# Decode attention with an MLP beside it: all sixteen K loads issued ahead of the V loads

## The chip, the cores and the metric

The kernel runs on one core of a Trainium2 chip. The metric is the device time of one execution in microseconds (us). Three runs of the kernel before took 236.51, 237.08 and 235.47 us; their median is 236.51 us. A further execution was profiled, and all durations below come from its trace.

## What is computed

The reference takes four tokens (a batch of 4, one position each, width 576), normalises them, and adds three things: the tokens themselves, a sliding-window attention against a K and a V cache, and a small mixer with an MLP. Cut to what matters:

```python
xn = layernorm(x)
# A: 32 query heads, 16 K/V heads, head width 128, window of the last 2048 of 8192 positions
q = (xn @ wq) ...                                # 576 x 4096
scores = einsum("bhqd,bhkd->bhqk", q, k) * Dh**-0.5
o = einsum("bhqk,bhkd->bhqd", softmax(scores), v)
A = o @ wo                                       # 4096 x 576
# B: two small products, then a 576 -> 4608 -> 576 MLP
h = gelu(layernorm(xn) @ w1);  x1 = xn + shift(h) @ w2
B = x1 + gelu(layernorm(x1) @ w3) @ w4
return x + A + B
```

Nearly all bytes are the two cache windows: 16 heads of K and 16 of V, 2 MB each for the four batch rows together. They and the weights make 88.90 MB of transfers in the profiled execution.

## The kernel before

**Work units.** One of the sixteen K/V heads is a group g. Its K tile (all four batch rows, 2048 positions, 128 wide) is one DMA of 2048 KB into one of three slots of `kring` (`NKU = 3`); its V tile is one such DMA into one of four slots of `vring` (`NVU = 4`).

**K stage.** For each group TensorE transposes the 64 blocks of 128x128 of the K tile in eight batches (`pe_T`, L324 to L332, signals `T{8g}` to `T{8g+7}`), ScalarE and VectorE copy the transposed batches out of PSUM (`evac`, L334 to L337), and TensorE multiplies them with the queries (`pe_SC`, L339 to L349). The scores of all sixteen groups gather in one PSUM region, each group's queries padded with zeros, so the softmax starts only when the last group's scores are in.

**Softmax.** A maximum over the scores (L365), four exponentials (L370), and a double transposition of the probabilities (L373, L378, L384 and L386) into the tile `PT`, about 15 us in all. Every PV product needs all of `PT`.

**V stage.** For each group, `pe_PV` (L398 to L408) runs 64 small matmuls with blocks of the V tile as the stationary operand. Beside them lie the mixer (L456 to L484) and, in three pieces, the output projection with `wo` (`pe_AO`, L426). At the end come the MLP's two products, with `w3` (`pe_h2`, L487) and `w4` (`acc_mm`, L424, called from L522).

**Order and queues.** Every engine's program is a list of steps with a hand-given key; the list is sorted by the key (L533) and emitted in that order. All big loads are issued by SyncE (SP) on one DMA queue, in the order of their keys. SP carries out its steps strictly one after the other: before a DMA whose slot or partner is not free, it waits on a semaphore, and nothing behind it is issued meanwhile. The waits around the change are:

- K of group g waits for the last transposition batch of group g-3, whose slot it takes (L209). K of groups 0 to 2 wait for nothing.
- V of groups 0 to 3 wait for the query projection only, since the query weights lie in the V slots at the start (L213). V of group g from 4 on waits for the PV product of group g-4.
- `wo` lands in the K slots and waits for `T127`, the last transposition of the K stage (L220 to L222). `w1` and `w2` follow it with no wait of their own (L223, L224), and then V of groups 4 to 15 (L225), `w3` (L228) and `w4` (L242).

The key of K of group g is g (L217). The key of V of group g below 4 is `G - V_EARLY + g - 0.5` (L219) with `G = 16` and `V_EARLY = 4`, which is 11.5, 12.5, 13.5 and 14.5: V0 stands behind K11, V1 behind K12, V2 behind K13 and V3 behind K14.

Of the kernel before, what the change touches and what calls it, by code (L numbers as in the profile page):

```python
# [14 lines left out]
V_EARLY = 4  # L15
# [21 lines left out]
def bass_parallel_sum__sliding_block_cached__mixer_s_mlp__decode_kernel(  # L37
# [8 lines left out]
    G = Hkv  # L46
# [11 lines left out]
    with ExitStack() as ctx:  # L58
# [95 lines left out]
        def add_dma(pairs, skey, waits=(), key=0.0, engine="sp"):  # L154
            if skey not in S:
                S[skey] = sem("s_" + "_".join(str(k) for k in (skey if isinstance(skey, tuple) else (skey,))))
            dma_count[skey] = dma_count.get(skey, 0) + 16 * len(pairs)

            def emit(e):
                for o_, i_ in pairs:  # L160
                    e.dma_start(o_, i_).then_inc(S[skey], 16)  # L161
            add(engine, emit, waits, None, key)
            return ("dma", skey, dma_count[skey])
# [41 lines left out]
        def kv_src(cache, g):  # L205
            return cache[:, g, Sk - W:Sk, :].rearrange("b (i t) d -> i b (t d)", t=NT)
# [5 lines left out]
        def issue_v(g, key):  # L212
            w = [f"PV{g - NVU}"] if g >= NVU else (["q"] if g < WQ_SLOTS else [])  # L213
            ev_v.append(add_dma([(vring_t[:, g % NVU * UE:(g % NVU + 1) * UE], kv_src(A_v_cache, g))], ("v", g % NVU), w, key))
# [1 line left out]
        for g in range(G):  # L216
            issue_k(g, g)  # L217
        for g in range(V_EARLY):
            issue_v(g, G - V_EARLY + g - 0.5)  # L219
        wo_wait = f"T{8 * (G - 1) + 7}"  # L220
        ev_wo = add_dma([(wo_sb.rearrange("p h r n -> p h (r n)"), A_wo.rearrange("(h p r) n -> p h (r n)", h=8, r=4))],
                        "wo", [wo_wait], KS)  # L222
# [15 lines left out]
        for c in range(8):  # L238
            g = G - NVU + c // 3
# [371 lines left out]
```

## Time and profile before

| what | number |
|---|---|
| median of three runs | 236.51 us |
| the profiled execution, its own time | 236.61 us |
| its span from the first to the last instruction | 234.9 us |
| moved by DMA | 88.90 MB, mean 378 GB/s over the span |
| TensorE busy | 169.7 us (72%) |
| VectorE busy | 74.3 us (32%) |
| ScalarE busy | 61.4 us (26%) |
| mean granted TensorE clock | 0.789 |

The profile gives all instants in us from the start of the span. The profiled execution's own time is 1.71 us longer than its span. Views used below are: the page's 40 equal slices of the span (a digit is a busy share in tenths; the GB/s row is what the DMA engines moved); the timeline of one engine's instructions; the chain of work that ended last, which names at each moment what the end of the program was waiting for; the table of waits; and a table of stretches between given instants, with busy time and count of each engine, the granted TensorE clock, the DMA engines' busy share and GB/s.

### The profile page before, as it was taken

Reading aid. Unit: us, or ns where it says so; the run is one execution under the profiler, and the core shown is the slowest. Engines: PE = TensorE matmul, PEld = TensorE weight load, DVE = VectorE, ACT = ScalarE, POOL = GpSimd, SP = SyncE. Lnnn points to the kernel's source line nnn. Section 1 sums busy time; section 2 is a strip of 40 time slices with the busy share of each in tenths; the row PEclk is TensorE's granted clock in tenths of the full one; section 3 lists DMA queues with packets and bytes.
Section 4 is the critical chain, followed back from the end, with each engine's and each line's share of the span. In section 5 each row is a group of like instructions: output and inputs, shape, how many; then the busy total and the mean of one; then the engine's idle time right before and its main releaser. Section 6 shows DMA issues by size and latency. Waiting matters only on the chain.

```text
span 234.9 us, 6181 instructions
## 1 busy us (share of the span) xinstructions
PE 169.7 (72%) x2917; PEld 126.3 (54%) x2918; DVE 74.3 (32%) x134; ACT 61.4 (26%) x74; POOL 6.1 (3%) x20
## 2 busy tenths in 40 slices
PE   0367999999999958396293479477498334994996
PEld 0355777777777646375161039444466334664753
DVE  4301566666565545143235850041000000000000
ACT  2001555555555534034234570002000000000000
POOL 8100000000000000000000000000000000000000
PEclk9999999999999999769978555555559555575569
DMA  7999999999999999999606997999999999999970
GB/s 258 421 433 435 413 399 385 419 373 407 410 393 399 419 430 424 427 435 426 276 0 224 418 390 307 416 427 438 413 430 438 413 433 424 428 433 393 410 314 10
DMA packets 8577, 88.90 MB, mean 378 GB/s; under 512 B 860, under 2 KB 1256, under 8 KB 3944
## 3 DMA queue, kind: packets, MB, share of 16 engines
q1 hardware_dynamic: 8536, 88.50, 90.9%
q8 instruction: 23, 0.38, 0.6%
q14 instruction: 2, 0.02, 0.0%
q10 hardware_dynamic: 16, 0.01, 0.0%
HBM read 88.49 MB, written 0.00 MB: 377 GB/s over the span
## 4 chain that ended last, share of the span: by engine, by line
DMA 51%; PE 37%; ACT 6%; DVE 3%; SPq 1%; issue 1%
DMA kring<-in_A_k_cache_dram 24%; PE ps L330 19%; DMA vring<-in_A_v_cache_dram 15%; DMA regB<-in_B_w_dram 12%; PE ps L346 6%; PE ps L424 5%; PE ps L403 5%; ACT regB L336 4%; ACT PT L384 1%; DVE PT L386 1%; PE ps L499 1%; SPq L161 1%; DVE rmax L365 1%; DVE regB L373 1%; PE ps L378 1%
## 5 line engine op out<-in xcount | busy, mean ns | idle before, releaser
L330 PE MATMUL ps<-perm_bf,kring 128*128 128x128 bf16 x1024 | 71.5, 229 | 14.9 <-DMA kring<-in_A_k_cache_dram 14.6
L330 PEld LDWEIGHTS ps<-perm_bf,kring 128*128 128x128 bf16 x1024 | 62.1, 103 | 29.4 <-DMA kring<-in_A_k_cache_dram 16.2
L337 DVE COPY regB<-ps 128x1024 bf16<-128x1024 bf16 x80 | 52.5, 687 | 54.9 <-PE ps L330 53.3
L336 ACT ACTIVATE regB<-ps 128x1024 bf16<-128x1024 bf16 x48 | 48.0, 1023 | 70.0 <-PE ps L330 70.0
L403 PE MATMUL ps<-PT,vring 128*128 128x8 bf16 x1024 | 29.2, 168 | 21.5 <-DMA vring<-in_A_v_cache_dram 20.3
L403 PEld LDWEIGHTS ps<-PT,vring 128*128 128x128 bf16 x1024 | 28.2, 103 | 24.8 <-DMA vring<-in_A_v_cache_dram 22.0
L346 PE MATMUL ps<-regB,Qpad 128*32 128x512 bf16 x256 | 18.4, 412 | 3.6 <-ACT regB L336 3.6
L514 ACT ACTIVATE h2T_sb<-ps 128x144 bf16<-128x144 f32 x1 | 0.3, 291 | 56.7 <-PE ps L508 56.7
L438 DVE TENSOR_TENSOR OTn<-ps,rinvB 128x64 bf16<-128x64 f32 (+2 forms) x3 | 0.6, 203 | 44.4 <-PE ps L403 44.4
L424 PE MATMUL ps<-kring,ORT 128*4 128x288 bf16 x64 | 13.4, 393 | 0.3 <-DVE ORT L442 0.3
L424 PE MATMUL ps<-vring,h2T_sb 128*4 128x288 bf16 x72 | 11.8, 339 | 0.5 <-ACT h2T_sb L514 0.5
L346 PEld LDWEIGHTS ps<-regB,Qpad 128*32 128x32 bf16 x256 | 5.6, 100 | 10.3 <-ACT regB L336 4.3
L378 PE MATMUL ps<-regB,permT 32*128 32x512 bf16 x16 | 5.9, 600 | 5.7 <-DVE regB L373 4.1
L424 PEld LDWEIGHTS ps<-kring,ORT 128*4 128x4 bf16 x64 | 7.0, 112 | 5.6 <-DVE ORT L442 0.4
L424 PEld LDWEIGHTS ps<-vring,h2T_sb 128*4 128x4 bf16 x72 | 7.1, 99 | 5.0 <-issue 0.5
L303 PE MATMUL ps<-xnT,vring 128*128 128x4 bf16 x160 | 4.6, 166 | 5.4 <-DMA vring<-in_A_wq_dram 5.4
L529 DVE CAST out_sb<-ps 4x288 bf16<-4x288 f32 x1 | 0.4, 446 | 23.6 <-PE ps L424 23.6
L499 PE MATMUL ps<-x1nT,regB 128*128 128x4 bf16 x144 | 5.0, 172 | 3.3 <-DMA regB<-in_B_w_dram 3.3
L303 PEld LDWEIGHTS ps<-xnT,vring 128*128 128x128 bf16 x160 | 4.4, 104 | 5.5 <-DMA vring<-in_A_wq_dram 5.5
L499 PEld LDWEIGHTS ps<-x1nT,regB 128*128 128x128 bf16 x144 | 4.9, 117 | 3.9 <-DMA regB<-in_B_w_dram 3.4
L378 PEld LDWEIGHTS ps<-regB,permT 32*128 32x128 bf16 x16 | 1.1, 99 | 10.5 <-DVE PT L386 5.3
L268 ACT ACTIVATE sd<-mv 4x1 f32<-4x1 f32 x3 | 0.6, 202 | 21.3 <-DVE mv L266 21.3
(82 smaller groups left out, 63.3 us busy)
## 6 DMA issues: line engine op xcount, KB each, us to landing
kring<-in_A_k_cache_dram SPq DMA_DIRECT2D x16, 2048.0 KB, 8.6
vring<-in_A_v_cache_dram SPq DMA_DIRECT2D x16, 2048.0 KB, 17.6
kring<-in_A_wo_dram SPq DMA_DIRECT2D x1, 4608.0 KB, 13.9
regB<-in_B_w_dram SPq DMA_DIRECT2D x2, 2304.0 KB, 25.8
vring<-in_B_w_dram SPq DMA_DIRECT2D x8, 576.0 KB, 28.4
vring<-in_A_wq_dram SPq DMA_DIRECT2D x2, 2048.0 KB, 9.6
kring<-in_B_w_dram SPq DMA_DIRECT2D x2, 576.0 KB, 15.1
regB<-in_B_w_dram SPq DMA_DIRECT2D x1, 576.0 KB, 29.9
```

The costliest lines, as they stand in the source:

```text
L161: e.dma_start(o_, i_).then_inc(S[skey], 16)
L303: ins = e.matmul(QTps[:, B * h:B * (h + 1)], lhsT=w, rhs=x_, start=(r == 0 and h == 0), stop=(r == 4), skip_group_check=True)
L330: ins = e.transpose(tb[n % NTB][:, t, :], kring[:, g % NKU, 8 * k + t, :], perm_bf[:])
L336: return "act", lambda e: e.activation(out=ktbuf[:, n % NKT], in_=tb[n % NTB], func=ACTF.Copy)
L337: return "dve", lambda e: e.tensor_copy(out=ktbuf[:, n % NKT], in_=tb[n % NTB])
L346: ins = e.matmul(Sps[32 * b:32 * b + 32, c4, :].rearrange("p (t i) -> p t i", t=16), lhsT=Qpad[:, g, b, :], rhs=kt[:, :, b, :], start=(g = ...
L365: add("dve", lambda e: e.tensor_reduce(out=rmax[:], in_=Sps, axis=AX.XY, op=ALU.max), waits=[f"SC{G - 1}"], sig="rmax", key=KS)
L373: add("dve", lambda e, cs=cs: e.transpose(PTc[:, cs], P_sb[:, cs]), waits=[f"exp{q}"], sig=f"PTc{q}", key=KS + 0.2 + 0.01 * q)
L378: add("pe", lambda e, m=m, q=q, b=b: e.matmul(PTps[m % 4], lhsT=permT[32 * b:32 * b + 32, :], rhs=PTc[32 * b:32 * b + 32, 512 * q:512 * q ...
L403: ins = e.matmul(OTps(g)[:, 8 * g:8 * g + 8].rearrange("p (b e) -> p b e", e=2), lhsT=vring[:, g % NVU, t, :], rhs=r_, start=(t == 0), sto ...
L424: return e.matmul(ACC[h], lhsT=lhsT, rhs=rhs, start=start, stop=stop)
L499: ins = e.matmul(H2Tps[:, n, :], lhsT=w3main[:, r, lo:hi:st], rhs=x1nT[:, r, :], start=(r == 0 and n == 0), stop=False, skip_group_check=True)
```

## The change

One line changes. The first four V loads get the keys 16, 17, 18 and 19 in place of 11.5 to 14.5, so that they stand behind K15 (key 15) and ahead of `wo` (key 132). No instruction is added or taken away, no wait, slot or semaphore differs, and the programs of TensorE, VectorE, ScalarE and GpSimd are the same.

```diff
         for g in range(G):
             issue_k(g, g)
         for g in range(V_EARLY):
-            issue_v(g, G - V_EARLY + g - 0.5)
+            issue_v(g, G + g)
         wo_wait = f"T{8 * (G - 1) + 7}"
```

SP's program before, from the query weights to `wo`. The x12 are K0 to K11; `waits prog_pe` is a wait for TensorE's progress.

```order
L161 DMA vring<-in_A_wq_dram 128x8192 x2
L161 DMA vring<-in_A_wq_dram 128x2048
L161 DMA kring<-in_A_k_cache_dram 128x1x8192 x3
L161 DMA kring<-in_A_k_cache_dram 128x1x8192 [waits prog_pe] x9
L161 DMA vring<-in_A_v_cache_dram 128x1x8192
L161 DMA kring<-in_A_k_cache_dram 128x1x8192 [waits prog_pe]
L161 DMA vring<-in_A_v_cache_dram 128x1x8192
L161 DMA kring<-in_A_k_cache_dram 128x1x8192 [waits prog_pe]
L161 DMA vring<-in_A_v_cache_dram 128x1x8192
L161 DMA kring<-in_A_k_cache_dram 128x1x8192 [waits prog_pe]
L161 DMA vring<-in_A_v_cache_dram 128x1x8192
L161 DMA kring<-in_A_k_cache_dram 128x1x8192 [waits prog_pe]
```

The four V loads alternate with K12 to K15. The same place in the changed program, up to the V loads behind `w2`:

```order
L161 DMA kring<-in_A_k_cache_dram 128x1x8192 x3
L161 DMA kring<-in_A_k_cache_dram 128x1x8192 [waits prog_pe] x13
L161 DMA vring<-in_A_v_cache_dram 128x1x8192 x4
L161 DMA kring<-in_A_wo_dram 128x8x2304 [waits prog_pe]
L161 DMA kring<-in_B_w_dram 128x2304
L161 DMA kring<-in_B_w_dram 128x288
L161 DMA kring<-in_B_w_dram 128x2304
L161 DMA kring<-in_B_w_dram 128x288
L161 DMA vring<-in_A_v_cache_dram 128x1x8192 [waits prog_pe] x12
```

K0 to K15 now stand together, and V0 to V3 lie between K15 and `wo`; they still wait for nothing of TensorE's.

## The prediction on record

> **What bounds the kernel now.** I read the page's slices first. One slice is 5.87 us long, and three rows of it, those of the TensorE clock, the DMA share and the GB/s, already tell most of the story.
>
> ```profile
> PEclk9999999999999999769978555555559555575569
> DMA  7999999999999999999606997999999999999970
> GB/s 258 421 433 435 413 399 385 419 373 407 410 393 399 419 430 424 427 435 426 276 0 224 418 390 307 416 427 438 413 430 438 413 433 424 428 433 393 410 314 10
> ```
>
> The DMA engines are busy in nearly every slice, so bytes bound the kernel, but there is a hole around slice 20 (near 120 us) in which nothing moves, and a dent at slice 24. There is also a long stretch, slices 5 to 12, where the engines count as busy and yet move about 400 GB/s and not 425 to 430. The table of stretches puts edges on these.
>
> ```profile
> 20.50:74.81 54.31, 52.33 (x788) 41.31 (x789) 32.71 (x50) 28.75 (x29) 0.00 (x0) 1.00 0.98 400
> 74.81:115.46 40.65, 28.43 (x400) 21.34 (x397) 16.51 (x26) 16.16 (x16) 0.00 (x0) 0.92 1.00 424
> 115.46:125.20 9.74, 6.81 (x80) 4.69 (x80) 3.27 (x5) 3.03 (x3) 0.00 (x0) 0.82 0.02 10
> 125.20:140.74 15.54, 8.47 (x89) 3.04 (x90) 11.10 (x18) 9.40 (x18) 0.00 (x0) 0.58 1.01 390
> 140.74:142.40 1.66, 1.66 (x68) 1.66 (x66) 0.00 (x0) 0.00 (x0) 0.00 (x0) 0.50 0.02 5
> 142.40:216.40 74.00, 48.68 (x1148) 37.70 (x1145) 5.09 (x18) 1.72 (x4) 0.00 (x0) 0.57 1.01 423
> ```
>
> The columns are the stretch and its length, busy us and count of PE, weight loads, DVE, ACT and POOL, then the granted clock, the DMA share and the GB/s. Two stops stand out: 9.74 us at a DMA share of 0.02, and 1.66 us at 0.02. What SP does then tells why.
>
> ```profile
> 74.81 0.53 SPq L161 DMA_DIRECT2D kring<-in_A_k_cache_dram  x1
> 75.39 0.60 SPq L161 DMA_DIRECT2D vring<-in_A_v_cache_dram  x1
> 80.15 0.54 SPq L161 DMA_DIRECT2D kring<-in_A_k_cache_dram  x1
> 85.50 0.54 SPq L161 DMA_DIRECT2D kring<-in_A_k_cache_dram  x1
> 93.14 0.53 SPq L161 DMA_DIRECT2D kring<-in_A_k_cache_dram  x1
> 124.21 0.40 SPq L161 DMA_DIRECT2D kring<-in_A_wo_dram  x1
> 141.11 45.58 SPq L161 DMA_DIRECT2D vring<-in_A_v_cache_dram  x12
> ```
>
> K12 to K15 are issued at 74.81, 80.15, 85.50 and 93.14. Then SP has nothing it may issue until 124.21, when the last transposition is done and `wo` may overwrite the K slots; all four V slots are full by then. And V4 goes out only at 141.11, when the first PV product has freed a slot, a little after the weights have run out at 140.74. The first stop is the costly one, and the chain of work that ended last says what holds `T127` back.
>
> ```profile
> 93.14 24.17 DMA kring<-in_A_k_cache_dram
> 117.36 1.81 PE ps L330 x16
> 123.56 0.63 PE ps L330 x8
> 139.23 3.55 PE ps L403 x128
> 146.84 17.79 DMA vring<-in_A_v_cache_dram
> 187.36 28.98 DMA regB<-in_B_w_dram
> 220.84 11.85 PE ps L424 x72
> ```
>
> K15 takes 24.17 us to arrive, because V1, V2, V3 and two K tiles lie ahead of it in one queue. Only at 117.36, after the queue has run dry, does TensorE get the last K tile; the softmax then runs to 139.23. From there V and w3 loads lead the chain, and the end is 11.85 us of matmuls with `w4`. TensorE's waits for K say the same.
>
> ```profile
> PE ps L330 <- DMA kring<-in_A_k_cache_dram: 1.2, 1, 1.2
> PE ps L330 <- DMA kring<-in_A_k_cache_dram: 13.4, 4, 4.7
> ```
>
> The first row is the window from 20 to 75 us, the second 75 to 125. Up to 75 us TensorE never waits for K but at the start: there it sets the pace, one group per 5.34 us (80.15 less 74.81), and SP issues K as slots come free. From the first early V on, each K tile is late.
>
> **The change, part by part.** No operation is added, so all is a matter of when bytes flow.
>
> *K12 to K15 come early.* K12 still goes out at 74.81, which is the end of group 9. With no V load ahead of it, it should land as those before did:
>
> ```profile
> kring<-in_A_k_cache_dram SPq DMA_DIRECT2D x16, 2048.0 KB, 8.6
> ```
>
> 8.6 us is the median from issue to landing, and a tile is needed two groups after its issue, 10.7 us, so about 2 us are spare. TensorE then keeps its 5.34 us for groups 10 to 15: K13 goes out at 80.15, K14 at 85.50, K15 near 90.84, and `T127` ends at 74.81 + 6 x 5.34 = 106.9 where it now ends at 124.2. TensorE's own 17.3 us are not the gain, since nothing waits for it but `wo` and the softmax.
>
> *V0 to V3 fill the hole.* SP issues them right behind K15, from 91.4 to 93.8 at 0.60 us each; the query projection they wait for is long done. How long do they keep the DMA engines busy? Between 74.81 and 115.46 these moved 40.65 x 0.424 = 17.24 MB, and the same bytes have to flow in the new order. Until K15 starts, TensorE paces them at the 400 GB/s of the first row of stretches. I put that start 1 us behind its issue, 91.84, as `wo` is issued at 124.21 and moves from 125.20. So 17.03 us carry 6.81 MB; the other 10.43 MB run freely.
>
> ```profile
> 80.00:115.00 35.00, 23.47 (x323) 17.58 (x320) 13.40 (x21) 13.20 (x13) 0.00 (x0) 0.90 1.01 427
> ```
>
> At 427 GB/s, the rate of the saturated part, 10.43 MB take 24.4 us, and V3's last bytes flow near 116.3 us. Against 115.46 the pacing **costs 0.85 to 0.96 us** (the second with 424 GB/s: 17.03 x 24 / 424). I take 0.96. The unknown is whether the 400 GB/s is pacing or the price of transposing beside the loads. The 427 row, with TensorE still busy 23.47 of 35 us, is nearer to pacing. If it is contention, V loads up to 106.9 run at 400 too and cost another 15.1 x 27 / 427 = 0.95 us; below nothing this term cannot go, for at best the rate is the free one.
>
> *The first stop goes.* `wo` may be issued from 106.9 on, some 9 us ahead of the end of V3. It queues behind V3 and starts without a pause: **9.74 us gained**. The cover is 9 us thick: if K15 or the last group is later than that, the stop comes back microsecond for microsecond.
>
> *The second stop goes.* PV of group 0 ends, and V4 is issued, 141.11 - 124.21 = 16.9 us after `T127`, so near 123.8 us. The weights `wo`, `w1` and `w2` flow from 116.4 to about 131 (15.54 us or a little less), so V4 is in the queue 7 us before it is needed, V5 to V7 soon after, each a PV product later: **1.66 us gained**. V0 to V3 must have landed for those PV products; the last does near 118.2, as K15's did 1.9 us (117.36 - 115.46) after the stream stopped, and PV0 starts at 106.9 + 139.23 - 124.21 = 121.9. Nothing is late next.
>
> *The starts after the stops go.* A stream that begins in an idle queue is slow at first:
>
> ```profile
> 125.20:126.00 0.80, 0.61 (x12) 0.39 (x16) 0.00 (x0) 0.78 (x2) 0.00 (x0) 1.00 0.99 115
> 126.00:140.00 14.00, 7.11 (x54) 1.91 (x46) 11.10 (x18) 8.23 (x17) 0.00 (x0) 0.56 1.02 408
> 142.40:144.00 1.60, 1.60 (x45) 1.54 (x43) 0.29 (x1) 0.00 (x0) 0.00 (x0) 0.50 1.01 348
> 144.00:216.40 72.40, 47.08 (x1109) 36.17 (x1106) 4.80 (x17) 1.72 (x4) 0.00 (x0) 0.57 1.01 425
> ```
>
> The weights' 15.54 x 0.390 = 6.06 MB at 408 GB/s take 14.9 us, 0.6 less; V4's first 1.60 us at 425 take 1.3, 0.3 less. Between nothing and 0.9 us, I take **0.5 us gained**: packets share the start and the end of a stream unevenly, so not all of that ramp need be lost time.
>
> *Behind V4* DMA bounds the program (1.01 share, 425 GB/s), the ring waits are the same, and the whole rest moves earlier as a block. In the last piece, TensorE's 11.85 us with `w4`, the clock decides.
>
> ```profile
> 222.00:224.00 2.00, 2.00 (x10) 1.10 (x9) 0.00 (x0) 0.00 (x0) 0.00 (x0) 0.50 1.02 412
> 228.00:230.00 2.00, 2.00 (x19) 1.40 (x17) 0.00 (x0) 0.00 (x0) 0.00 (x0) 1.00 0.22 81
> ```
>
> At clock 0.50 ten matmuls run in 2 us, at 1.00 nineteen. Should it come up never, 72 of them take 14.4 us, 2.6 more; should it be up from the start, the last `w4` bytes, flowing until about 229.5, hold the gain near 2. I take no change, as that stretch starts from the same kind of wait.
>
> **Sum**: 9.74 + 1.66 - 0.96 + 0.5 = 10.9 us. From the profiled execution's 236.61 us (1.71 above its span) that gives **225.7 us**; the median of the runs shown, 236.51, is 0.1 below the profiled one, which changes nothing.
>
> **The rivals.**
>
> *The second stop stays, and the loads are slowed beside TensorE.* If V4 still went out after the weights had run out, or the 400 GB/s were contention, 1.66 and 0.95 us would be missing, and no ramp gained: 225.7 + 1.66 + 0.95 + 0.5 = 228.8 us. For it: 400 GB/s at a DMA share of 0.98 looks like a busy engine. Against: V4 has 7 us to spare, and K at one tile per 5.34 us cannot come faster than it does.
>
> *The K stage loses its clock.* After a wait of 4.70 us TensorE ran one group at a reduced clock:
>
> ```profile
> 97.80:105.82 8.02, 7.79 (x80) 5.88 (x80) 3.33 (x5) 2.05 (x2) 0.00 (x0) 0.62 1.00 423
> ```
>
> That is 8.02 us against 5.34. If groups 10 to 15, now a block with no pause, all ran so, `T127` would fall at 74.81 + 6 x 8.02 = 122.9, K15 would go out near 98.9, V3 would end near 125, `wo` would start where it does now, and of the stops only the second would shrink, V4 being issued at 139.8 and not at 141.11: about 235 us, no change within 1%. Against it: the first row of stretches has the granted clock at 1.00 for 54 us of this very work. The Trainium skill ("TensorE: Matmul & The Clock Gate", section "Part 4: PE-mode transpose") says that the full clock does not engage for transposes, since they do not count as TensorE activity in the same way. By that rule a longer block of transposing would go cold and this rival's 235 us would be the time; the trace disagrees with it, with 1.00 over 788 matmuls, most of them transposes, so I give it little.
>
> *The queue shares its rate (slower).* Five tiles, K15 and V0 to V3, are then open at once. If the DMA engines served open transfers side by side, K15 would land only with V3, 1.9 us after 116.3, so at 118.2 and not at 117.36. `T127` would follow 6.85 us later as now (124.21 - 117.36), near 125.1; both stops stay, and all comes 0.8 to 0.9 us later: 237.5 us. The point from which it decides is K15 landing after about 109 us (then `wo` is late for its cue), and it turns to a loss past 117.4. Against it: with V0 to V3 open too, K12 to K15 landed one by one, two tiles (about 9.8 us) apart, which is what a queue in order gives.
>
> ```profile
> 87.89 1.07 PE L330 MATMUL ps<-perm_bf,kring 128*128 128x128 bf16 x16 [2.42 <-DMA kring<-in_A_k_cache_dram]
> 97.81 1.89 PE L330 MATMUL ps<-perm_bf,kring 128*128 128x128 bf16 x16 [4.70 <-DMA kring<-in_A_k_cache_dram]
> 107.59 1.07 PE L330 MATMUL ps<-perm_bf,kring 128*128 128x128 bf16 x16 [1.77 <-DMA kring<-in_A_k_cache_dram]
> ```
>
> **How the numbers follow.** A measurement of this kernel can tell about 1% from no change. My forecast of 225.7 us gets 0.82, the weaker gain at 228.8 us 0.09, the lost clock 0.04, the shared queue 0.04, and 0.01 is left for a loss I do not see. The first two are faster by over 1% (4.6% and 3.3%): 0.92 with a rounding; the third and fourth lie within 1%: 0.07; slower 0.01. The forecast's own range goes from 225.7 - 0.4 - 1.8 (all ramps gained, and most of what a higher clock can give at the end) = 223.5 to the weaker gain, 228.8, which also takes in a last piece wholly at half clock (228.3). That leaves out about 2 in 10.
>
> **What would show it.** Right: K12 to K15 issued 5.3 to 5.4 us apart; `wo` issued near 107; no waits of TensorE for K between 75 and 107; no slice of the DMA row below 9 between 10 and 220 us; V4 issued near 124 and flowing from about 131; w3 read by TensorE near 205.5 where it was 216.4. Wrong: a K tile landing more than 11 us after its issue, a clock below 0.9 between 75 and 107 us, or a hole in the GB/s row between V3 and `wo` or between `w2` and V4. A gain below 7 us would mean that the block behind V4 does not move as one.

## The result and the profile after

The changed kernel took 225.32 us (median of 4 runs, 224.30 to 227.49) against 236.8 us for the kernel before (four runs now; the fourth took 238.81): the ratio is 0.952, 95% interval 0.942 to 0.963. Here and below a median is that of all runs, and a ratio leaves out the runs that were over 1.5% slower than the fastest of their kernel. Two further rounds of measurement on other occasions gave 224.5 and 224.44 us, with ratios of 0.951 (0.947 to 0.955) and 0.956 (0.951 to 0.962). The forecast was 225.7 us. The profiled execution took 224.30 us, with a span of 222.5 us.

The page's slices of the changed kernel, in the order in which they were shown for the kernel before (one slice is 5.56 us now):

```profile
PEclk9999999999999999999955555555569555585589
DMA  6999999999999999999999999999999999999991
GB/s 236 424 445 439 424 386 404 395 386 390 392 407 395 409 383 380 409 417 424 424 427 401 410 426 424 421 439 421 424 421 427 427 427 427 426 431 396 408 373 55
```

The hole and the dent are gone: no slice from the second to the second last is under 9 in the DMA row. TensorE's clock no longer drops inside the K stage. The low stretch of the GB/s row, in which K is asked for at TensorE's pace, is longer now: slices 5 to 15, counted from 0, instead of 5 to 12. SP's timeline shows what is issued when:

```profile
74.80 16.57 SPq L161 DMA_DIRECT2D kring<-in_A_k_cache_dram  x4
91.41 2.57 SPq L161 DMA_DIRECT2D vring<-in_A_v_cache_dram  x4
106.87 0.39 SPq L161 DMA_DIRECT2D kring<-in_A_wo_dram  x1
107.30 12.96 SPq L161 DMA_DIRECT2D kring<-in_B_w_dram  x4
123.78 52.52 SPq L161 DMA_DIRECT2D vring<-in_A_v_cache_dram  x12
```

K12 to K15 go out within 16.57 us, V0 to V3 right behind them, `wo` at 106.87 and V4 at 123.78. The table of stretches (length, busy us of PE, weight loads, DVE, ACT and POOL, the granted clock, DMA share, GB/s) has no stop left between these:

```profile
74.81:91.80 16.99, 16.21 (x256) 12.44 (x253) 10.38 (x17) 9.84 (x11) 0.00 (x0) 1.00 0.99 395
91.80:106.90 15.10, 14.46 (x224) 10.86 (x224) 9.25 (x15) 7.95 (x10) 0.00 (x0) 1.00 1.00 412
106.90:116.40 9.50, 3.35 (x23) 0.79 (x23) 6.39 (x10) 5.06 (x10) 0.00 (x0) 0.69 1.01 426
116.40:131.00 14.60, 11.18 (x267) 8.15 (x267) 5.04 (x11) 5.29 (x8) 0.00 (x0) 0.50 1.01 408
131.00:205.00 74.00, 44.84 (x1009) 33.64 (x1006) 4.80 (x17) 1.72 (x4) 0.00 (x0) 0.57 1.01 425
```

The chain of work that ended last closes with these two pieces:

```profile
176.99 28.25 DMA regB<-in_B_w_dram
209.75 10.56 PE ps L424 x72
```

The second half of `w3` arrives at 205.24 us (176.99 + 28.25), where it came at 216.34 (187.36 + 28.98): 11.1 us earlier. The last piece takes 10.56 us and not 11.85, 1.3 us less. Together these are the 12.4 us by which the span shrank.

### The profile page after: what moved, and what is told of

Its sections match the earlier page's. It is cut to its first block, busy times and chain, and to the rows that moved or that the text cites. A ratio compares the mean times of both kernels' runs of the same rounds, so it can differ in the third digit from the quotient of the medians.

```text
span 222.5 us, 6182 instructions
## 1 busy us (share of the span) xinstructions
PE 164.8 (74%) x2918; PEld 123.3 (55%) x2918; DVE 74.0 (33%) x134; ACT 60.9 (27%) x74; POOL 6.0 (3%) x20
## 4 chain that ended last, share of the span: by engine, by line
PE 44%; DMA 39%; ACT 10%; DVE 3%; issue 2%; SPq 1%
PE ps L330 24%; DMA vring<-in_A_v_cache_dram 18%; DMA regB<-in_B_w_dram 13%; DMA kring<-in_A_k_cache_dram 8%; PE ps L346 8%; ACT regB L336 7%; PE ps L403 5%; PE ps L424 5%; ACT PT L384 2%; DVE PT L386 1%; PE ps L499 1%; SPq L161 1%; DVE rmax L365 1%; DVE regB L373 1%; PE ps L378 1%
## 5 line engine op out<-in xcount | busy, mean ns | idle before, releaser
L330 PE MATMUL ps<-perm_bf,kring 128*128 128x128 bf16 x1024 | 68.3, 224 | 1.3 <-DMA kring<-in_A_k_cache_dram 1.2
L330 PEld LDWEIGHTS ps<-perm_bf,kring 128*128 128x128 bf16 x1024 | 59.6, 100 | 14.6 <-issue 6.4
L336 ACT ACTIVATE regB<-ps 128x1024 bf16<-128x1024 bf16 x48 | 47.5, 1022 | 53.1 <-PE ps L330 53.1
L346 PE MATMUL ps<-regB,Qpad 128*32 128x512 bf16 x256 | 16.8, 382 | 4.5 <-ACT regB L336 4.5
L424 PE MATMUL ps<-vring,h2T_sb 128*4 128x288 bf16 x72 | 10.5, 315 | 0.5 <-ACT h2T_sb L514 0.5
L424 PEld LDWEIGHTS ps<-vring,h2T_sb 128*4 128x4 bf16 x72 | 6.5, 92 | 4.2 <-issue 0.5
L476 DVE TENSOR_TENSOR x_bf<-ps,xn_bf 4x288 bf16<-4x288 f32 x2 | 0.9, 446 | 18.0 <-PE ps L471 18.0
```

The lines of the kernel that those rows point to most:

```text
L330: ins = e.transpose(tb[n % NTB][:, t, :], kring[:, g % NKU, 8 * k + t, :], perm_bf[:])
L336: return "act", lambda e: e.activation(out=ktbuf[:, n % NKT], in_=tb[n % NTB], func=ACTF.Copy)
L346: ins = e.matmul(Sps[32 * b:32 * b + 32, c4, :].rearrange("p (t i) -> p t i", t=16), lhsT=Qpad[:, g, b, :], rhs=kt[:, :, b, :], start=(g = ...
L424: return e.matmul(ACC[h], lhsT=lhsT, rhs=rhs, start=start, stop=stop)
```

## The experiments

There are two theories to tell apart. **Theory A**, that of the prediction: the DMA stream bounds the program and the gain is the removal of its two stops. **Rival B**: the gain comes from the K stage and the softmax ending 17.3 us earlier, and the order of the other loads is incidental. Both fit the trace of the changed kernel, since the change brought both things about.

**V behind the weights.** All K stay first, but V0 to V3 go behind `w2`, so that `T127` is as early as in the changed kernel and the stream has nothing to do while TensorE ends the K stage.

```diff
-            issue_v(g, G + g)
+            issue_v(g, KS + 0.3 + 0.01 * g)
```

> V0 to V3 stand behind w2 instead of behind K15; the K stage is that of the changed kernel, with T127 at 106.9 us. Theory A (the gain is the removal of the stops in the DMA stream): K15's bytes end near 96.7 us and wo cannot start before 107.9, so a stop of about 11 us is back, only at an earlier place; V4 flows near 143 us where the changed kernel has 131: about 237 us (236 to 238.5). Rival B (the gain is the earlier end of the K stage and of the softmax): T127 and PT are as early as in the changed kernel, so the time stays at 225.3 us, at most 1.5 us more.

It took 235.8 us (10 runs), just under the range forecast for theory A, a ratio to the kernel before of 1.000 (0.998 to 1.003). SP's timeline and two stretches of it:

```profile
107.04 0.39 SPq L161 DMA_DIRECT2D kring<-in_A_wo_dram  x1
109.89 77.14 SPq L161 DMA_DIRECT2D vring<-in_A_v_cache_dram  x16
```

```profile
97.50:98.50 1.00, 1.00 (x18) 0.36 (x19) 0.00 (x0) 0.80 (x1) 0.00 (x0) 1.00 0.14 57
98.50:108.00 9.50, 8.28 (x128) 6.52 (x128) 5.85 (x9) 4.94 (x5) 0.00 (x0) 1.00 0.01 3
```

`wo` goes out at 107.04 us, 17.2 us earlier than in the kernel before, and the whole gain is gone: the DMA engines stand still for 9.5 us at a share of 0.01 and run at 0.14 in the microsecond before. The second half of `w3` arrives at 216.68 us, 11.4 us later than in the changed kernel. Rival B falls. An early end of the K stage is worth nothing in itself here; what counts is that something is in the queue while it ends.

**TensorE late by 15 us and by 5 us.** Matmuls of zeros are put between the transpositions of groups 14 and 15 in the changed kernel, to see how thick the covers of `wo` and V4 are.

```diff
+        def pe_pad(e):
+            for w in range(69):
+                e.matmul(ps[:, 7, :], lhsT=zeros_bf[:, 0:128], rhs=zeros_bf[:, :], start=True, stop=True)
+        add("pe", pe_pad, waits=["xn2T"], key=8 * (G - 1) - 0.1)
         for g in range(G):
             add("pe", pe_SC(g)
```

> The changed kernel with 69 such matmuls (about 15 us of TensorE) at the same place. T127 moves to about 121.8 us, past the cover of 9 us. Theory A: wo flows from 122.8 and not from 116.3, a stop of 6.5 us; V4 is issued near 138.7 and flows from 140 where it was 131: 9 us longer, 234.3 us (233 to 236). Rival B: the full 15 us longer, 240. If nothing but bytes counted: 225.3.

It took 233.31 us (4 runs). From SP's timeline and the stretches:

```profile
121.52 0.39 SPq L161 DMA_DIRECT2D kring<-in_A_wo_dram  x1
121.95 2.99 SPq L161 DMA_DIRECT2D kring<-in_B_w_dram  x4
138.42 45.40 SPq L161 DMA_DIRECT2D vring<-in_A_v_cache_dram  x12
```

```profile
117.00:122.00 5.00, 4.48 (x70) 3.18 (x67) 3.19 (x5) 2.52 (x3) 0.00 (x0) 1.00 0.06 23
138.00:139.00 1.00, 1.00 (x44) 1.00 (x41) 0.00 (x0) 0.00 (x0) 0.00 (x0) 0.50 0.06 16
```

Both stops are back, at the places forecast: one ahead of `wo`, one ahead of V4. Of 14.65 us by which `wo` was issued later (121.52 less 106.87), about 8 us reached the end (233.31 less 225.32), where 9 were forecast; rival B wanted all of it.

With 23 matmuls in the place of 69:

> The changed kernel with 23 matmuls of zeros (about 5 us of TensorE) between the groups 14 and 15 of transpositions; their output is not read. T127 moves to about 112 us. Theory A: wo is still issued 4 us ahead of the end of V3, and V4 near 128.8, 2 us ahead of the end of the weights; both covers hold and the time stays at 225.3 us (224.5 to 226). Rival B: 5 us longer, 230.3.

The median was 226.75 us, the ratio 0.949 (0.940 to 0.959). With 5 runs between 224.1 and 229.9 us that leaves open whether a microsecond is missing, so it was measured again, beside the changed kernel:

> About 5 us of TensorE between the groups 14 and 15 once more, in more rounds. Theory A (covers of 9 us for wo and 7 us for V4): equal to the changed kernel on the same chip within 0.7 us. Rival B: 5 us above it.

> The changed kernel as it is, to stand beside the others on the same chip: 225.3 us (224 to 227.5 in single runs).

225.56 us (224.41 to 226.96) stood against 224.5 us (223.91 to 225.68) of the changed kernel, 6 runs each; the ratios to the kernel before are 0.955 (0.950 to 0.959) and 0.951 (0.947 to 0.955). Three stretches of the delayed kernel, around the places at which the stops had lain (V3 to `wo` near 116 us, `w2` to V4 near 131):

```profile
107.00:116.00 9.00, 5.57 (x87) 3.60 (x84) 5.40 (x6) 4.35 (x4) 0.00 (x0) 1.00 1.01 431
116.00:131.00 15.00, 9.28 (x137) 4.45 (x138) 8.92 (x18) 8.07 (x16) 0.00 (x0) 0.53 1.01 407
131.00:200.00 69.00, 45.18 (x1065) 34.95 (x1065) 5.09 (x18) 1.72 (x4) 0.00 (x0) 0.57 1.01 426
```

All are full, at a DMA share of 1.01. TensorE's timeline of the delayed kernel and, in the second fence, of the changed one:

```profile
205.45 2.52 PE L503 MATMUL ps<-x1nT,regB 128*128 128x4 bf16 x72 [2.15 <-DMA regB<-in_B_w_dram]
209.93 11.83 PE L428 MATMUL ps<-vring,h2T_sb 128*4 128x288 bf16 x72 [0.47 <-ACT h2T_sb L518]
```

```profile
206.57 2.52 PE L499 MATMUL ps<-x1nT,regB 128*128 128x4 bf16 x72 [1.93 <-DMA regB<-in_B_w_dram]
211.04 10.64 PE L424 MATMUL ps<-vring,h2T_sb 128*4 128x288 bf16 x72 [0.47 <-ACT h2T_sb L514]
```

In these two profiles `w3` is no later in the delayed kernel, and the other two profiles of the changed kernel have it at 205.28 and 205.38 us. What differs is the last piece, 11.83 us against 10.64. So both covers hold for 5 us. The medians' 1.1 us is more than the 0.7 us I allowed, though the intervals overlap; rival B's 5 us it is not.

**Is 400 GB/s in the K stage TensorE's pace, or a price of transposing beside the loads?** The prediction took pace. If so, TensorE with less to do must let K flow faster. This kernel leaves out 12 of the 16 score matmuls of the groups 1 to 14, so its scores are those of a part of the window only; all transpositions and copies stay.

```diff
-                for c4 in range(4):
+                for c4 in (range(4) if g in (0, G - 1) else (3,)):
```

> The changed kernel, with three quarters of the score products of groups 1 to 14 left out (4 matmuls instead of 16; all transpositions and copies stay). TensorE then needs about 4.55 us a group, less than a K tile takes on a free queue (4.9 us). If the 400 GB/s of the K stage are TensorE's pace, the K stage runs at 420 GB/s or more, with waits for K, and the end comes 3 to 4 us earlier: about 221.5 us. If the loads are slowed by the transposing beside them, the rate stays near 400 GB/s, TensorE waits for K some 0.6 us a group, and the time stays at 225 us (224 to 226).

It took 223.4 us (4 runs), a ratio to the kernel before of 0.944 (0.940 to 0.949). Its stretches, and those of the changed kernel in a third measurement, which took 224.44 us (6 runs):

```profile
37.00:60.00 23.00, 20.53 (x313) 16.68 (x309) 14.45 (x23) 13.93 (x14) 0.00 (x0) 1.00 0.99 399
60.00:75.00 15.00, 14.20 (x216) 11.48 (x213) 10.29 (x17) 9.47 (x10) 0.00 (x0) 1.00 1.00 422
75.00:92.00 17.00, 15.54 (x231) 12.39 (x229) 11.23 (x18) 10.63 (x11) 0.00 (x0) 1.00 1.01 425
```

```profile
37.00:60.00 23.00, 21.88 (x348) 16.90 (x348) 14.27 (x22) 13.04 (x14) 0.00 (x0) 1.00 0.97 395
60.00:75.00 15.00, 14.54 (x231) 11.12 (x224) 9.12 (x14) 7.86 (x9) 0.00 (x0) 1.00 1.00 397
75.00:92.00 17.00, 16.10 (x257) 12.33 (x258) 10.50 (x16) 9.86 (x11) 0.00 (x0) 1.00 0.98 394
```

From 60 us on the loads run at 422 to 425 GB/s beside the same transpositions, and TensorE waits for K instead, 6.9 us in 12 waits, the first of them at the start. That alone would leave the score matmuls that were left out as a cause. The changed kernel itself settles it. K15 landed near 99.6 us (issued at 90.84, 8.8 us to landing), and from then on V loads, which wait for nothing of TensorE's, flow beside the last groups of the K stage:

```profile
102.00:106.90 4.90, 4.61 (x71) 3.24 (x68) 3.20 (x5) 2.52 (x4) 0.00 (x0) 1.00 1.00 425
```

TensorE is busy for 4.61 of 4.90 us with the transpositions and score matmuls of the full kernel, and the loads run at 425 GB/s, as they do in the same stretch of the third measurement. So it is pace and not a price of TensorE's work.

The end came only 1.0 to 1.9 us earlier than in the three measurements of the changed kernel, not 3 to 4, and the intervals of the ratios (0.947 to 0.955 for the changed kernel measured beside it) overlap. One part of that stands in the rows: up to 60 us the rate was still 399. TensorE's first wait for K after the start came late:

```profile
46.92 1.07 PE L330 MATMUL ps<-perm_bf,kring 128*128 128x128 bf16 x16 [0.74 <-DMA kring<-in_A_k_cache_dram]
```

Until then it used up tiles that had already landed, a group every 4.70 us. Why the loads did not speed up in that stretch, though slots came free sooner, stays open.

**One V load in the gaps of the pace.** If pace leaves gaps, a V load early in the K stage might use them.

```diff
-            issue_v(g, G + g)
+            issue_v(g, (5.5, G + 1, G + 2, G + 3)[g])
```

> V0 stands behind K5, V1 to V3 behind K15 as in the changed kernel. If the 400 GB/s of the K stage are TensorE's pace (K asked for at one tile per 5.34 us), V0 uses the gaps: K6 comes some 2.5 to 3 us late once, T127 moves from 106.9 to about 110 us, still 4 us ahead of the end of V3, and the stream ends about 2 us earlier: 223.3 us (222.5 to 224). If the 400 GB/s are the price of transposing beside the loads, there are no gaps: 225.3 us, with T127 near 111.8. Rival B, by which the end follows the K stage: 228 us or more.

226.02 us (4 runs, 223.66 to 227.04; ratio 0.953, 0.944 to 0.963) decided nothing, so it was measured again, beside the changed kernel's 224.5 us.

> V0 behind K5 once more, in more rounds. If it filled gaps that the pace leaves, it would be 2 us below the changed kernel on the same chip. If the K stage has no gaps to fill, it is equal to it or up to 1 us above; the first runs (median 226.0) speak for this.

227.06 us (225.60 to 228.56, 6 runs), a ratio to the kernel before of 0.962 (0.957 to 0.966), whose interval lies above that of the changed kernel (0.947 to 0.955). This early V load costs about 1%, and both of my expectations were too kind to it. Its table of waits and two stretches:

```profile
PE ps L330 <- DMA kring<-in_A_k_cache_dram: 4.0, 2, 2.6
```

```profile
37.00:60.00 23.00, 19.68 (x282) 14.34 (x280) 10.87 (x17) 10.93 (x11) 0.00 (x0) 0.89 1.01 419
60.00:75.00 15.00, 14.33 (x216) 11.76 (x215) 9.21 (x14) 7.27 (x8) 0.00 (x0) 0.93 0.93 371
```

At first the load does fill gaps (419 GB/s against 408 for the changed kernel measured beside it, and 395 in the rows of its third measurement above). But K6 comes late, TensorE waits 2.6 us and loses clock (0.89, then 0.93), its requests come later, and the rate falls to 371 GB/s at a DMA share of 0.93. By these rows the gaps are moved, not filled. `wo` went out at 112.08 us, so its cover shrank too. The profiled execution was the fastest of the six, so the trace does not show where the rest of the loss lies; that stays open.

**The last piece.** Its 72 matmuls took 11.84 us in the profile of before and 10.54 in that of after, with part of the time at half clock. One stretch of before and, under it, one of after:

```profile
226.00:228.00 2.00, 2.00 (x16) 1.25 (x14) 0.00 (x0) 0.00 (x0) 0.00 (x0) 0.82 0.71 281
210.00:216.00 6.00, 6.00 (x39) 3.67 (x38) 0.00 (x0) 0.00 (x0) 0.00 (x0) 0.75 1.00 401
```

The clock steps from 0.50 to 1.00 within each. Means of 0.82 and 0.75 put the step near 226.7 and 213.0 us, 5.9 and 3.2 us after the piece began (at 220.84 and 209.75). That fits the 1.3 us between the two pieces: the later piece ran 2.7 us more at half clock, at which ten matmuls take the time of nineteen at 1.00. Could TensorE be kept at full clock by filling its waits?

```diff
+        def pe_keep(k):
+            def f(e):
+                for w in range(k):
+                    e.matmul(ps[:, 3, :], lhsT=zeros_bf[:, 0:128], rhs=zeros_bf[:, :], start=True, stop=True)
+            return f
+        add("pe", pe_keep(8), waits=["rinvB"], key=KT + 1.5)
+        add("pe", pe_keep(2), key=KT + 10)
```

> The changed kernel, with ten matmuls of zeros that keep TensorE busy: eight while it waits for the second half of w3, two while it waits for the last activation; their output is not read. The last piece, 72 matmuls with w4, took 11.84 us in the profile of before, 10.54 and 10.64 in two of the changed kernel, 11.83 in two of experiments, always with part of it at half clock. If the clock sets that piece, it falls to 9 us or less, held then by the last w4 bytes, and the time falls by 1.5 to 2.5 us to about 222.7. If the w4 loads set it, nothing changes: 224.5. If the filling only delays the products with w3: up to 1 us longer.

> The changed kernel as it is, beside the one that keeps the clock: 224.5 to 225.3 us.

226.48 us stood against 224.44 us, with ratios of 0.962 (0.957 to 0.967) and 0.956 (0.951 to 0.962): not shorter, and whether it is longer the overlapping intervals leave open. From the stretches and TensorE's timeline of its profiled execution, at 229.06 us the longest of the six:

```profile
208.00:216.00 8.00, 8.00 (x127) 5.32 (x126) 0.00 (x0) 0.29 (x1) 0.00 (x0) 0.50 1.02 409
```

```profile
205.81 3.57 PE L519 MATMUL ps<-zeros_bf 128*128 128x512 bf16 x8
213.95 11.19 PE L424 MATMUL ps<-vring,h2T_sb 128*4 128x288 bf16 x72
```

TensorE is busy for 8.00 of 8.00 us and the granted clock stays at 0.50: these matmuls of zeros do not bring it up, and at half clock the eight take 3.57 us and hold up the products with `w3`. What a full clock from the start would do to the last piece was therefore not tried; nothing here beats the changed kernel with the whole computation in it.

## Why the prediction was right, point by point

- **K early, TensorE at its own pace: right.** 16.57 us for four issues is three times 5.34 us and one issue. `wo` at 106.87 us was forecast for 106.9. TensorE's table of waits has none for K after 75 us.
- **The first stop goes, with a cover of 9 us: right.** The second, with a cover of 7 us: right; V4 went out at 123.78 (forecast: near 123.8). The 15 us delay brought both back and the 5 us delay did not bring back either. How much each stop gave by itself was not measured apart.
- **The pacing cost, taken at 0.96 us, was a little small.** From 74.81 to 116.40 the changed kernel moved 16.99 x 0.395 + 15.10 x 0.412 + 9.50 x 0.426 = 16.98 MB. The 17.24 MB of the kernel before were through near 117.0 us and not at 116.4, which makes the cost 1.5 us. The sum let the pace end at 91.84, where K15 starts; but K15 itself still ran at the pace. The 412 GB/s of the second stretch are a mean: 400 up to 97.00, 411 up to 102.00 and 425 after that. The lower end of the cost in the prediction, 0.85, should read 0.81 by its own numbers (91.84 + 10.43 / 0.427 - 115.46); the sum does not use it.
- **The slow starts were worth more than the 0.5 us I took.** By the arrival of `w3` the gain is 11.1 us; 9.74 + 1.66 - 1.5 are 9.9, so about 1.2 us are left for the two starts, above my upper bound of 0.9. This is a remainder of the sum and was not measured by itself. That this term was 0.7 too small and the pacing cost 0.5 too small, so that the two nearly cancel, is luck.
- **The block behind V4 moves as one: right.** `w3` was read at 205.28 us, forecast near 205.5.
- **The last piece, taken at no change, gave 1.3 us** in the profiled execution, inside the bounds stated. It hangs on when the clock comes up, and in the profile of the kernel delayed by 5 us it was 11.83 us, so this is not a gain of the change that can be counted on.
- **The rivals.** The lost clock did not come: the granted clock was 1.00 from 74.81 to 106.90, over 480 matmuls and now without a pause. The shared queue did not come: K15 landed 8.8 us after its issue, with V0 to V3 open behind it, and `wo` went out on time. The weaker gain at 228.8 us supposed contention or a second stop; V loads ran at 425 GB/s beside the K stage, and the second stop is gone.

## What to carry to other kernels

In a program that DMA bounds, look for the instants at which its engines have nothing queued, and ask which waiting issue ends each of them. A load that waits for nothing is the means to fill such a hole, so it belongs behind the loads that somebody waits for and ahead of the issue that stalls. Spent early, between loads that TensorE waits for, it delays these and then is missing when the stall comes. Moving work earlier gained nothing by itself here: the kernel with the early K stage and the empty queue was as slow as before (1.000, 0.998 to 1.003).

## What the runs showed of the hardware that was not expected

- The DMA busy share does not tell a full queue from a paced one: in the changed kernel 394 to 397 GB/s came with shares of 0.97 to 1.00, and the same loads ran at 422 to 425 GB/s with shares of 1.00 to 1.01 once TensorE asked sooner.
- Ten matmuls of zeros of 128x512, with small matmuls between them, did not raise the granted clock in the one execution profiled: it stayed at 0.50 over 8 us in which TensorE was never idle. Put into a stage whose clock stood at 1.00, 69 of them in a row left it there (1.00 over the 15.06 us that they took).
- A DMA stream that starts from an empty queue costs more than the idle time it shows, by about 1.2 us for two starts, as far as the sum can tell.
